# Key-value products of the next batch but one, moved from the first layer of the network to the second

## The chip, the cores and the metric

The kernel runs on one core of a Trainium2 chip. The metric is the device time of one execution, in microseconds. TensorE (PE) multiplies, VectorE (DVE) and ScalarE (ACT) work element by element, GpSimd (POOL) and SyncE (SP) here issue DMAs.

## The reference, cut to what matters

```python
def _attn_ref(q, k, v, g_norm):             # q, k, v: (8, 8, 576, 64)
    kv = np.einsum('bhsd,bhse->bhde', k, v)
    out = np.einsum('bhsd,bhde->bhse', q, kv)
    rms = np.sqrt(np.mean(out * out, axis=-1, keepdims=True) + 1e-06)
    return out / rms * g_norm

def _moe_ref(x, w_in, w_out):                # 4608 tokens, 512 -> 2048 -> 512
    h = x @ w_in
    g = h * (1.0 / (1.0 + np.exp(-1.702 * h)))
    return g @ w_out

# x = the attention's output of all batches, (batch, position) x (head, channel)
```

## The kernel before, in words

There are eight batches and nine tiles of 512 tokens. The loop at the end of the kernel runs over `t` from 0 to 8: pass `t` (called layer t here) puts tile `t` through both layers of the network, and beside it does the attention of batch `t + 1`. Tiles 0 to 7 hold the first 512 positions of a batch, tile 8 the last 64 positions of all of them. The weights stay in SBUF in f16.

**The network.** From layer 1 on both products are done as block products with seven multiplications instead of eight. The first half of a layer (`hid_seven`, `SevenIn`, L559) has 28 products of four 128x256 matmuls, in an order written out by hand: `SECOND` for layer 1, `LATER` for layers 2 to 6, `LAST_TWO` for 7 and 8. A step "21" is product 1 of group 2. The word "kv" in that list is the place of the key-value product. Product 1 of each group is followed by a copy of its bank to the bank on which product 2 accumulates (`snap`, L509, by ScalarE "A" or VectorE "D"). The gates, ScalarE's activations at L539, write `gT`; VectorE forms sums of operands (`xS` L491, `gS` L611). The second half (`Seven.run`, L681) has seven products of 16 matmuls in the order 1, 5, 6, 2, 7, 3, 4; a step of it is one matmul, so there are 112. Products 1, 6, 7 and 4 share one bank: after 1, 5 and 6 `keep` copies the state of a bank to `qf` (ScalarE, L648), and the next product goes on accumulating. `place` writes the output tile `osb` (VectorE L656; the last product's by ScalarE, L659).

**The attention.** For batches 2 to 7, `kv_all` makes k-transposed times v for four pairs of heads (40 matmuls, L238) into one bank and copies it to `kvd` in four copies of 64x256 (L509); before all are VectorE's. `kvd` has two buffers, by the parity of the batch. In the second half, behind step 15 in layers 2 to 6 (`'rows': (15, 15)`), `rows` makes two sets of 128 rows of q times kv with each call (L313, 16 matmuls a call), and ScalarE squares them. `add_up` sums the squares (VectorE, L329), `roots` takes roots (ScalarE, L338), `turn` scales and hands pairs of row sets to a DMA transpose into `xT`, the operand of the next layer. The last 64 positions go through `out`, `ss` and `apply`. The squares go through three buffers:

```python
sq = attn.tile([P, SM], F16, name="sq", tag="sq", bufs=3)
```

Each engine takes its instructions in the order in which the program was written; there is no scheduler. `at1(i, ...)` puts work behind step i of the first half, `at2(i, ...)` behind step i of the second; the late product "34" of `LATER`, with its gate, also stands behind step 15, ahead of the work put there. There is one buffer each for k and v (`kraw`, `vbuf`), so their next load, from GpSimd's queue, follows the product that reads them. q has two.

Of the kernel before, what the change touches and what calls it, by code (L numbers as in the profile page):

```python
# [7 lines left out]
F16 = mybir.dt.float16  # L8
# [4 lines left out]
P = 128  # L13
# [3 lines left out]
def kernel(  # L17
# [10 lines left out]
    nc = tc.nc  # L28

    B, H, S, D = q.shape  # L30
    DM = H * D
    DFF = moe_w_in.shape[1]
    NPAIR = H // 2
    FO = DFF // P
    KO = DM // P
    EPS = 1e-6
    SM = 512
    J = SM // P
# [10 lines left out]
    const = ctx.enter_context(tc.tile_pool(name="const", bufs=1))  # L49
    stage = ctx.enter_context(tc.tile_pool(name="stage", bufs=4))  # L50
    attn = ctx.enter_context(tc.tile_pool(name="attn", bufs=4))
# [18 lines left out]
    ident = const.tile([P, P], F16)  # L70
    ones2 = const.tile([P, P], F16)
    eps_t = const.tile([P, 1], F32)
    g_col = const.tile([P, 1], F32)
    w_in_sb = const.tile([P, KO, DFF], F16)
    w_out_sb = const.tile([P, FO, DM], F16)
# [32 lines left out]
    RW = J * D  # L108
    RS = H * RW

    def load_kv(b, h0=0, h1=H, rest=True):

        for n in "kv":
            nc.gpsimd.dma_start(  # L114
                out=kv_rows[n][:, h0 * RW : h1 * RW].rearrange("p (h x) -> p h x", x=RW),
                in_=srcs[n][b, h0:h1, 0:SM, :].rearrange("h (p j) d -> p h (j d)", j=J),
            )
        for n in "kv" if rest else "":
            nc.gpsimd.dma_start(
                out=kv_rows[n][0:R, RS : RS + H * D].rearrange("p (h d) -> p h d", d=D),  # L120
                in_=srcs[n][b, :, SM:S, :].rearrange("h p d -> p h d"),
            )

    def clear_rest():
        for n in "kv":
            nc.vector.memset(kv_rows[n][R:P, RS : RS + H * D], 0.0)
# [19 lines left out]
    for n in "kqv":  # L146
        if n != "q":
            rows = stage.tile([P, 6, 2 * P], F32, name="qf", tag="qf", bufs=2)
            rows = rows.rearrange("p h x -> p (h x)")[0:PE_]
# [8 lines left out]
        out=ident,  # L158
        in_=ident,
# [42 lines left out]
    xT = {}  # L202
# [8 lines left out]
    class Attention:  # L211
# [3 lines left out]
        def __init__(self, b):  # L215
            self.b, self.kb = b, kvb[b] if b < EARLY else kvd[b % 2]
            self.qT, self.o = {}, {}
            x = xpool.tile([P, KO * SM], F16, name="xT", tag="xT")
            if b < EARLY:
                self.x = xT[b] = x.rearrange("p (c n) -> p c n", c=KO)  # L220
            else:
                self.x = x.rearrange("p (m r) -> p m r", r=P)
                xT[b] = x.rearrange("p (j c r) -> p c j r", j=J, c=KO)
                self.x16 = attn.tile([P, J, DM], F16, name="x16", tag="x16", bufs=1)

        def kv(self, c):
            if c % self.KEEP == 0:
# [35 lines left out]
        def keep_kv(self, c0, c1):  # L263

            for half in range(2):
                to = slice(half * D, (half + 1) * D)
                for hl in range(2):
                    r = slice(hl * D, (hl + 1) * D)
                    copy(self.engine, self.kb[to, c0:c1, half, 1 - hl], self.kvp[r, c0:c1, :])

        def transpose_q(self):
            self.qTd = attn.tile([P, H * J // 2, P], F16, name="qTd", tag="qTd", bufs=1)
# [65 lines left out]
            nc.scalar.activation(s4, s4, AFT.Abs_reciprocal_sqrt, bias=eps_t, scale=1.0 / D)  # L338

        def turn(self, j):  # L340
            nc.vector.tensor_mul(
                self.x16[:, j, :].rearrange("p (h d) -> p h d", d=D),
                self.o[j][0].rearrange("p (h d) -> p h d", d=D),
                self.sum4[:, j, :].unsqueeze(2).to_broadcast([P, H, D]),
            )
            if j % 2:
                nc.sync.dma_start_transpose(
                    out=self.x[:, (j - 1) * KO : (j + 1) * KO, :],
                    in_=self.x16[:, j - 1 : j + 1, :].rearrange("p j n -> p (j n)"),
                )  # L350
# [157 lines left out]
    def copy(engine, to, src):  # L508
        (nc.vector.tensor_copy if engine == "D" else nc.scalar.copy)(to, src)  # L509
# [347 lines left out]
    for hl in range(2):  # L857
        r = slice(hl * D, (hl + 1) * D)
# [91 lines left out]
    def plan(t):  # L950
        return SECOND if t < EARLY else LATER if t < B - 1 else LAST_TWO
# [7 lines left out]
    for t in range(NT):  # L959
        b = t + 1  # L960
        u1, u2 = {}, {}

        def at1(i, f, *args):
            u1.setdefault(i, []).append(lambda: f(*args))

        def at2(i, f, *args):
            u2.setdefault(i, []).append(lambda: f(*args))  # L967

        def of(b, name, *args):
            return lambda: getattr(live[b], name)(*args)  # L970

        if t == 0:
            for l in range(2):
                at1(6, nc.vector.memset, kvd[l], 0.0)
            at1(7, of(0, "out", NPAIR))
            at1(7, scale_w_in, 0, 4)
            at1(7, w_in_sums, 0, 2)
            at1(8, start, 1)
            at1(12, scale_w_in, 4, 6)
            at1(12, w_in_sums, 2, 3)  # L980
            at1(13, load_q, 2)
            at2(4, setattr, a0, "ss_pool", Attention.ss_pool)
            at2(4, of(0, "ss", NPAIR, True))
            at2(4, of(0, "apply", NPAIR))
            at2(18, weight_sum, 0, 0, HF)
            at2(18, scale_w_in, 6, 8)
            at2(18, w_in_sums, 3, 4)
            for c in range(NPAIR):
                at1(12, of(1, "pack_q", c))
                at2(9 + 3 * c, of(1, "q", c))  # L990
                at2((36, 37, 49, 50)[c], of(1, "kv", c))
                at2((41, 43, 54, 55)[c], of(1, "out", c))
                at2((45, 50, 58, 60)[c], of(1, "ss", c))
                at2((48, 52, 58, 62)[c], of(1, "apply", c))
            for n in range(1, 4):
                at2(19, weight_sum, n, 0, 4)
                at2(38, weight_sum, n, 4, 6)
            at2(39, load_kv, 2, 0, H // 2, False)
            at2(51, clear_rest)
            at2(51, load_kv, 2, H // 2, H)  # L1000

            def first_sum():
                made[1] = Sums(1, xT[1])
                made[1].form(0)

            at2(55, first_sum)
        elif b < B:
            todo = plan(t)
            at1(todo.steps.index("kv"), of(b, "kv_all", todo.keep))
            if t == 1:  # L1010
                at1(5, start, b)
                at1(5, of(b, "transpose_q"))
                at1(4, nc.scalar.preload_act_table_set, "gelu_apprx_sigmoid_and_others")
                for n, i in ((1, 8), (2, 11), (3, 16)):
                    at1(i, weight_sum, n, 6, HF)
            if t + 2 < B:
                late = max(15, todo.steps.index("kv") + 1)
                at1(late, load_kv, t + 2)
                at1(late, load_q, t + 2)
                at2(100, start, t + 2)  # L1020
                at2(100, of(t + 2, "transpose_q"))
            at = todo.attn
            at2(at["table"], nc.scalar.preload_act_table_set, "abs_reciprocal_sqrt_and_small")
            for h in range(2):
                at2(at["roots"][h], of(b, "roots", h))
            for j in range(J):
                if j < J // 2:
                    at2(at["rows"][j], of(b, "rows", j))
                for name in ("add_up", "turn"):
                    at2(at[name][j], of(b, name, j))  # L1030
            at2(46, of(b, "out", NPAIR))
            at2(74, of(b, "ss", NPAIR))
            at2(80, of(b, "apply", NPAIR))
            at2(82, nc.scalar.preload_act_table_set, "gelu_apprx_sigmoid_and_others")
        elif t < B:
            for name in ("ss_pool", "rest_pool"):
                at2(16, setattr, live[1], name, (ps_a, "att"))
            at2(16, of(1, "out", NPAIR))
            at2(34, nc.scalar.preload_act_table_set, "abs_reciprocal_sqrt_and_small")
            at2(44, of(1, "ss", NPAIR))  # L1040
            at2(50, of(1, "apply", NPAIR))
            at2(52, nc.scalar.preload_act_table_set, "gelu_apprx_sigmoid_and_others")
        layers(t, u1, u2)
# [30 lines left out]
```

## Time and profile before

| | us |
|---|---|
| median of 3 runs | 260.13 (260.03 to 260.14) |
| profiled execution, its own time | 260.59 |
| its span, first to last instruction | 258.8 |
| TensorE busy | 251.4 (97%) |
| VectorE busy | 195.1 (75%) |
| ScalarE busy | 174.9 (68%) |
| GpSimd busy | 53.8 (21%) |

Busy times are shares of the span. A wait of one engine counts only if it lies on the chain that ended last. The chain here is 92% TensorE. Layer 2 lasts from 74.39 to 100.61 us, layer 3 to 126.82, and the layers up to 6 follow at the same distance; layers 7 and 8, without key-value products, are shorter up to the final store.

### The profile page before, as it was taken

What the parts mean: (1) busy time and instruction counts of PE and PEld (TensorE: products, weight loads), DVE (VectorE), ACT (ScalarE), POOL (GpSimd) and SP (SyncE); (2) the same over time, 40 slices, a digit from 0 to 9 for tenths busy, and PEclk for the clock granted to TensorE, in tenths of its full rate; (3) what the DMA queues carried; (4) which work ended last, traced back from release to release, by engine and by line L of the source; (5) the groups of instructions that cost most, each with busy time, mean ns of one, the idle gap of its engine ahead of it and who ended that gap; (6) DMA issues with size and microseconds to landing.
All of it is one profiled execution on the core that took longest, in us unless ns stands there. A gap on an engine that the chain in (4) does not pass through costs nothing.

```text
span 258.8 us, 6349 instructions
## 1 busy us (share of the span) xinstructions
PE 251.4 (97%) x2596; PEld 203.7 (79%) x2596; DVE 195.1 (75%) x351; ACT 174.9 (68%) x315; POOL 53.8 (21%) x81
## 2 busy tenths in 40 slices
PE   8889999999999999999999999999999999999993
PEld 2434454788888888888888888888888888888882
DVE  1565685899968896899689968996899687557842
ACT  3378734988749974997489748984798569737820
POOL 8773245107026001600170007000000000000001
PEclk9999999999999999999999999999999999999999
DMA  7999999999989957996799579947600610021005
GB/s 169 192 196 205 205 204 197 218 214 124 175 182 150 226 66 154 159 214 79 167 152 221 65 177 149 228 50 178 160 4 0 172 73 3 0 89 77 3 0 162
DMA packets 68559, 35.33 MB, mean 136 GB/s; under 512 B 37874, under 2 KB 65778, under 8 KB 68402
## 3 DMA queue, kind: packets, MB, share of 16 engines
q0 software_dynamic: 37520, 18.17, 54.4%
q1 hardware_dynamic: 30688, 16.36, 26.9%
q8 instruction: 20, 0.33, 0.5%
q10 hardware_dynamic: 322, 0.39, 0.4%
q14 instruction: 9, 0.07, 0.1%
HBM read 36.70 MB, written 9.44 MB: 178 GB/s over the span
## 4 chain that ended last, share of the span: by engine, by line
PE 92%; DMA 4%; DVE 1%; issue 0%; ACT 0%; POOL 0%
PE o L681 38%; PE h L559 38%; PE o L795 6%; PE hT L452 5%; DMA qraw<-in_q_dram 2%; DMA vbuf<-in_v_dram 2%; PE kvp L238 2%; PE outR L313 1%; PE ss L358 1%; PE kvp L250 0%; PE outT L283 0%; PE q L433 0%; DVE xT L368 0%; PE outT L287 0%; ACT rs L360 0%
## 5 line engine op out<-in xcount | busy, mean ns | idle before, releaser
L539 ACT ACTIVATE gT<-h 128x512 f16<-128x512 f32 x96 | 52.5, 602 | 5.4 <-PE h L559 5.4
L559 PEld LDWEIGHTS <-ws 128*128 128x128 f16 x512 | 50.1, 98 | 5.8
L681 PEld LDWEIGHTS <-gS 128*128 128x128 f16 x512 | 49.4, 98 | 6.2 <-DVE gS L611 0.3
L559 PE MATMUL h<-xS,ws 128*128 128x256 f16 x384 | 52.2, 273 | 0.0
L681 PE MATMUL o<-tw,gS 128*128 128x256 f16 x384 | 46.5, 273 | 0.0
L681 PEld LDWEIGHTS <-gT 128*128 128x128 f16 x384 | 37.6, 98 | 4.3
L559 PEld LDWEIGHTS <-w_in_sb 128*128 128x128 f16 x384 | 37.1, 98 | 4.7
L559 PE MATMUL h<-xT,w_in_sb 128*128 128x256 f16 x224 | 31.9, 273 | 0.0
L681 PE MATMUL o<-w_out_sb,gT 128*128 128x256 f16 x256 | 31.4, 273 | 0.0
L573 DVE TENSOR_TENSOR h<-h,s 128x512 f32<-128x512 f32 x32 | 22.2, 698 | 6.8 <-PE h L559 5.5
L575 DVE TENSOR_TENSOR s<-h,s 128x512 f32<-128x512 f32 x32 | 22.1, 692 | 4.1 <-PE h L559 3.3
L656 DVE TENSOR_TENSOR osb<-o,qf 128x512 f32<-128x512 f32 (+1 forms) x25 | 16.7, 668 | 11.2 <-PE o L681 8.3
L114 POOL DMA_DIRECT2D kraw<-in_k_dram x7 | 6.0, 853 | 90.6 <-PE kvp L238 86.4
L611 DVE TENSOR_TENSOR gS<-gT 128x512 f16<-128x512 f16 (+2 forms) x32 | 21.3, 686 | 0.6 <-ACT gT L539 0.6
L539 ACT ACTIVATE gT<-s 128x512 f16<-128x512 f32 x32 | 19.8, 628 | 2.6 <-DVE s L575 2.6
L714 POOL DMA_DIRECT2D out_dram<-osb x2 | 1.1, 562 | 92.0 <-DVE osb L656 92.0
L559 PE MATMUL h<-xS,w_in_sb 128*128 128x256 f16 x128 | 18.9, 273 | 0.0
L360 ACT ACTIVATE rs<-ss,eps_t 128x512 f32<-128x512 f32 (+1 forms) x16 | 9.2, 581 | 13.8 <-PE ss L358 13.7
L967 ACT ACT_TABLE_LOAD x14 | 18.0, 1283 | 0.2
L648 ACT COPY qf<-o 128x512 f32<-128x512 f32 (+1 forms) x26 | 14.2, 547 | 4.5 <-PE o L681 4.3
L329 DVE TENSOR_REDUCE sum<-sq 128x8 f32<-128x512 f16 x24 | 15.3, 678 | 2.5 <-ACT sq L323 2.5
L509 ACT COPY h<-h 128x512 f32<-128x512 f32 x27 | 15.7, 586 | 2.1 <-PE h L559 2.0
(100 smaller groups left out, 362.9 us busy)
## 6 DMA issues: line engine op xcount, KB each, us to landing
out_dram<-osb SPq DMA_DIRECT2D x10, 512.0 KB, 3.6
kraw<-in_k_dram POOLq DMA_DIRECT2D x5, 512.0 KB, 9.2
vbuf<-in_v_dram POOLq DMA_DIRECT2D x5, 512.0 KB, 12.1
qraw<-in_q_dram POOLq DMA_DIRECT2D x3, 512.0 KB, 13.2
qbuf<-in_q_dram POOLq DMA_DIRECT2D x3, 512.0 KB, 13.4
out_dram<-osb SPq DMA_DIRECT2D x6, 192.0 KB, 6.2
w_in_sb<-in_moe_w_in_dram POOLq DMA_DIRECT2D x2, 512.0 KB, 10.7
w_out_sb<-in_moe_w_out_dram POOLq DMA_DIRECT2D x2, 512.0 KB, 15.3
```

The costliest lines, as they stand in the source:

```text
L329: nc.vector.tensor_reduce(out=self.sum4[:, j, :], in_=self.o[j][1].rearrange("p (x d) -> p x d", d=D), op=ALU.add, axis=mybir.AxisListType.X,)
L509: (nc.vector.tensor_copy if engine == "D" else nc.scalar.copy)(to, src)
L539: nc.scalar.activation(self.gT[:, to, n * TH : (n + 1) * TH], src, AFT.Gelu_apprx_sigmoid)
L559: nc.tensor.matmul(bank[name][:, a], w, x, start=(p in (1, 5) and a == 0 and k == 0), stop=(k == KH - 1), skip_group_check=True,)
L573: nc.vector.tensor_add(bank["z"], bank["x"], self.s5)
L575: nc.vector.tensor_add(self.s5, bank["x"], self.s5)
L611: op(s[:, n, lo], a, b)
L648: nc.scalar.copy(self.kept[as_][:, m], ps)
L656: nc.vector.tensor_add(o, ps, self.kept[with_][:, m])
L681: nc.tensor.matmul(o, a, w, start=(p in (1, 2, 5) and i == 0 and (mo == 0 or split)), stop=(i == HF - 1), skip_group_check=True,)
L795: nc.tensor.matmul(os[mo], gT[:, fo, mo * P : (mo + 1) * P], w_out_sb[:, fo, :], start=(fo == 0), stop=(fo == FO - 1),)
L967: u2.setdefault(i, []).append(lambda: f(*args))
```

## The change

The key-value product of batch 2 stays in the first half of layer 1. That of batch 3 moves to step 95 of the second half of layer 1; those of batches 4 to 7 move to step 15 of the second half of layers 2 to 5, ahead of the rows of batches 3 to 6. In the first halves of layers 2 to 6 nothing stands at "kv" any more. The four copies take letters of their own, "DDDD", "DADA" and "ADDD", instead of one letter for all. k of the next batch is loaded right behind the product; v, the rests and q wait on GpSimd behind `after_turn`, a copy of one element of the transposed rows. The squares' sum of the last positions, its application and the table load move from steps 74, 80 and 82 to 82, 88 and 90. The buffer `x16` is taken in the first `turn` instead of with the batch's object.

```diff
-    def load_kv(b, h0=0, h1=H, rest=True):
+    def load_kv(b, h0=0, h1=H, rest=True, main="kv"):
-        for n in "kv":
+        for n in main:
             nc.gpsimd.dma_start(
...
+    def after_turn(b):
+        nc.gpsimd.tensor_copy(out=mark, in_=xT[b].rearrange("p c j r -> p j c r")[0:1, J - 1, KO - 1, 0:1])
...
-                    copy(self.engine, self.kb[to, c0:c1, half, 1 - hl], self.kvp[r, c0:c1, :])
+                    copy(
+                        self.engine[2 * half + hl],
+                        self.kb[to, c0:c1, half, 1 - hl],
+                        self.kvp[r, c0:c1, :],
+                    )
...
-            at1(todo.steps.index("kv"), of(b, "kv_all", todo.keep))
+            at = todo.attn
             if t == 1:
+                at1(todo.steps.index("kv"), of(b, "kv_all", "DDDD"))
...
+                at1(22, load_kv, 3)
+                at1(22, load_q, 3)
+                at2(95, start, 3)
+                at2(95, of(3, "kv_all", "DADA"))
+                at2(96, load_kv, 4)
+                at2(96, load_q, 4)
+            elif t + 2 < B:
+                at2(at["rows"][0], start, t + 2)
+                at2(at["rows"][0], of(t + 2, "kv_all", "ADDD"))
+                if t + 3 < B:
+                    at2(at["rows"][0], load_kv, t + 3, 0, H, False, "k")
+                    at2(101, after_turn, b)
+                    at2(101, load_kv, t + 3, 0, H, True, "v")
+                    at2(101, load_q, t + 3)
             if t + 2 < B:
-                late = max(15, todo.steps.index("kv") + 1)
-                at1(late, load_kv, t + 2)
-                at1(late, load_q, t + 2)
-                at2(100, start, t + 2)
                 at2(100, of(t + 2, "transpose_q"))
...
-            at2(74, of(b, "ss", NPAIR))
-            at2(80, of(b, "apply", NPAIR))
-            at2(82, nc.scalar.preload_act_table_set, "gelu_apprx_sigmoid_and_others")
+            at2(82, of(b, "ss", NPAIR))
+            at2(88, of(b, "apply", NPAIR))
+            at2(90, nc.scalar.preload_act_table_set, "gelu_apprx_sigmoid_and_others")
```

More of the change, by code (lines that the diff above doesn't have):

```diff
@@ L72 @@
     eps_t = const.tile([P, 1], F32)
+    mark = const.tile([1, 1], F16)
     g_col = const.tile([P, 1], F32)
@@ L223, in __init__ @@
                 xT[b] = x.rearrange("p (j c r) -> p c j r", j=J, c=KO)
-                self.x16 = attn.tile([P, J, DM], F16, name="x16", tag="x16", bufs=1)
         def kv(self, c):
@@ L340, in turn @@
         def turn(self, j):
+            if j == 0:
+                self.x16 = attn.tile([P, J, DM], F16, name="x16", tag="x16", bufs=1)
             nc.vector.tensor_mul(
@@ L1015 @@
                     at1(i, weight_sum, n, 6, HF)
+                at1(22, load_kv, 3)
[12 more added lines that the diff above has]
+                    at2(101, load_q, t + 3)
             if t + 2 < B:
-                late = max(15, todo.steps.index("kv") + 1)
-                at1(late, load_kv, t + 2)
-                at1(late, load_q, t + 2)
-                at2(100, start, t + 2)
                 at2(100, of(t + 2, "transpose_q"))
-            at = todo.attn
             at2(at["table"], nc.scalar.preload_act_table_set, "abs_reciprocal_sqrt_and_small")
```

## The prediction

> **What bounds the kernel now.** I read the page first, then the stretches of one layer each, then who made TensorE wait.
>
> ```profile
> span 258.8 us, 6349 instructions
> PE 251.4 (97%) x2596; PEld 203.7 (79%) x2596; DVE 195.1 (75%) x351; ACT 174.9 (68%) x315; POOL 53.8 (21%) x81
> PEclk9999999999999999999999999999999999999999
> 100.61:126.82 26.21, 26.21 (x303) 23.18 (x302) 22.01 (x38) 19.41 (x36) 5.27 (x7) 1.00 1.04 153
> 126.82:153.04 26.22, 26.22 (x304) 23.20 (x302) 22.02 (x38) 19.41 (x36) 5.27 (x7) 1.00 0.99 151
> ...
> PE kv L250 <- DMA vbuf<-in_v_dram: 0.9, 2, 0.7
> PE hT L452 <- DVE xT L368: 0.3, 1, 0.3
> ```
>
> A middle layer lasts 26.2 us, and TensorE is busy in all of it (the first number after the stretch is its length, the second TensorE's busy time). The waits for TensorE name only lines of the start (L250, L452). So a layer is a queue of matmuls with no hole. The change adds and drops no matmul: six key-value products are made before and after. The time can only fall by cheaper neighbours in that queue, and it rises by every hole that opens. The question is therefore which matmul now comes before its operands are ready.
>
> The stretches that matter, from the timeline of one layer (start, length, engine, line; a matmul's length holds its drain, so starts are what to read):
>
> ```profile
> 100.44 1.04 PE L559 MATMUL h<-xT,w_in_sb 128*128 128x256 f16 x8
> 101.41 0.82 PE L238 MATMUL kvp<-vbuf,kraw 128*64 128x64 f16 x40
> 102.17 0.61 PE L559 MATMUL h<-xT,w_in_sb 128*128 128x256 f16 x4
> ...
> 114.84 0.60 PE L559 MATMUL h<-xS,w_in_sb 128*128 128x256 f16 x4
> 115.37 0.64 PE L313 MATMUL outR<-kvd,qTd 64*128 64x64 f16 x32
> 115.94 3.56 PE L681 MATMUL o<-tw,gS 128*128 128x256 f16 x31
> ...
> 121.31 1.36 PE L681 MATMUL o<-tw,gS 128*128 128x256 f16 x11
> 102.23 11.02 PE h L559 x100
> ```
>
> The last row, from the chain, gives 0.11 us for one 128x256 matmul.
>
> **Part 1: the key-value product leaves the first half of layers 2 to 6.** It stood behind the first two products of the plan, "21 01 kv 22". It filled 0.76 us (102.17 - 101.41) and some 0.10 us of entry: eight matmuls from 100.44 last 0.87, and the product began at 101.41 instead of 101.31. Product 22 accumulates onto a bank that ScalarE first fills with a copy of product 21 (the plan's snap for group 2 is "A"). ScalarE's rows at that place:
>
> ```profile
> 100.64 0.58 ACT L659 COPY osb<-o 128x512 f32<-128x512 f32 x1 [2.27 <-PE o L681]
> 101.13 0.59 ACT L509 COPY h<-h 128x512 f32<-128x512 f32 x1
> ```
>
> The copy that 22 needs (L509) stands behind the copy of the old layer's last output (L659), which itself waits for that layer's last matmul. It ends at 101.13 + 0.59 = 101.72. Before, 22 came at 102.17 and the key-value product hid this. Now 22 follows directly at 101.31, while the copy still ends at 101.72; with 0.04 us for the handover (the rows show 0.02 to 0.04 from one engine's end to another's start) TensorE stands until 101.76, a hole of 0.45 us. It occurs in layers 2 to 6: 5 x 0.45 = 2.25 us. What else is late there? VectorE loses its four casts (1.7 us), so its sums come no later.
>
> **Part 2: the product stands ahead of the rows in layers 2 to 5.** The rows began at 115.37 and took 0.57 us. In their place come 40 small matmuls. What stays is the body, and the step from one small kind to the other replaces the step back to a large matmul and the entry to the rows. No row shows that step. It lies between nothing (the spacing inside either group) and a full entry of 0.10 more than usual; the exit from the key-value product is 0.76 less 20 pairs of about 0.03, some 0.13. I take 0.11 us saved a layer, nearer to the entry seen at 101.41; the ends are 0 and 0.2. The Trainium skill, "TensorE: Matmul & The Clock Gate", section "Part 3: Packing small matmuls — row/col tiling", says that a weight load overlaps running matmuls only where the row groups differ; the product uses all 128 rows, so by it nothing would be saved and the sum would be 0.44 us higher. The rows inside the product speak for more overlap than that: 40 weight loads and 40 matmuls, all on the same 128 rows, start within 0.63 us.
>
> What follows on the other engines is the larger matter. The rows of before:
>
> ```profile
> 115.52 0.60 ACT L539 ACTIVATE gT<-h 128x512 f16<-128x512 f32 x1
> 116.01 2.08 ACT L323 ACTIVATE sq<-outR 128x512 f16<-128x512 f32 x4
> 118.10 1.28 ACT L967 ACT_TABLE_LOAD   x1
> 119.40 0.31 ACT L338 ACTIVATE sum<-sum,eps_t 128x16 f32<-128x16 f32 x1
> 119.61 0.57 ACT L648 COPY qf<-o 128x512 f32<-128x512 f32 x1
> 120.08 0.31 ACT L338 ACTIVATE sum<-sum,eps_t 128x16 f32<-128x16 f32 x1
> 120.28 0.37 ACT L301 ACTIVATE sq<-outT 128x256 f16<-128x256 f32 x1
> 120.55 0.58 ACT L648 COPY qf<-o 128x512 f32<-128x512 f32 x1
> ...
> 115.48 0.69 DVE L611 TENSOR_TENSOR gS<-gS,gT 128x1024 f16<-128x1024 f16 x1
> 116.65 1.28 DVE L329 TENSOR_REDUCE sum<-sq 128x8 f32<-128x512 f16 x2 [0.47 <-ACT sq L323]
> 117.84 0.68 DVE L611 TENSOR_TENSOR gS<-gT,gS 128x1024 f16<-128x1024 f16 x1
> 102.46 1.72 DVE L509 CAST kvd<-kvp 64x256 f16<-64x256 f32 x4
> L648 ACT COPY qf<-o 128x256 f32<-128x256 f32 x4 | 1.5, 371 | 0.8 <-PE o L681 0.8
> L238 PE MATMUL kvp<-vbuf,kraw 128*64 128x64 f16 x240 | 4.9, 197 | 0.0
> ```
>
> ScalarE is full from 115.52 to 121.13, the end of the last copy to qf. TensorE needs that copy: the product that begins at 121.31 goes on accumulating in the bank which it reads. So before there are 0.18 us to spare. Now, with the layer's clock up to 115.37 as before:
>
> 1. The product's last matmul starts at 115.37 + 0.63 and ends 0.20 later, 116.20.
> 2. The four copies out of its bank carry the letters "ADDD". In the order of the changed program ScalarE's copy is first, and VectorE's first one waits for it. ScalarE on this shape is not in the trace; its nearest row, 256 columns, is 0.37 us, its 512-column copy 0.58. With 0.37: 116.23 to 116.60.
> 3. VectorE's three: 3 x 0.43 (1.72 / 4) from 116.63, so it is free at 117.92. Queued behind them are a sum for the second half (L611, 0.60 to its successor) and the first reduction of squares, which so begins at 118.52 and ends at 119.20. It was at 116.65.
> 4. Only three buffers hold squares ("bufs=3"). ScalarE's fourth square must wait for that reduction: 119.25 instead of 117.45 (116.01 + 3 x 0.48).
> 5. Behind this on ScalarE stand the table load, both roots and both copies to qf, the rest as full as before: 121.13 - 117.45 = 3.68 us, so the last copy ends at 122.93, and TensorE may go on at 122.97.
> 6. TensorE itself would be there at 121.31 + 0.75 = 122.06. Hole: 0.91 us, in four layers 3.64 us.
>
> The turned rows are late by the same 1.8 us, but the layer's end moves by 0.75 + 0.91, so the transposes keep their distance to the next layer within 0.2 us. With ScalarE at 0.58 in step 2 a layer costs 0.2 more.
>
> **Part 3: batch 3's product near the end of layer 1, and the loads.** Layer 1 gains 0.86 us, which layer 2's first half loses: nothing in sum. Its copies alternate VectorE and ScalarE, each behind the other, some 1.8 us beside 17 matmuls (1.9 us); cover that just suffices. The squares' sum, its application and the table load move eight steps back, into ScalarE's idle end of the layer; nothing.
>
> ```profile
> 103.39 0.90 POOL L114 DMA_DIRECT2D vbuf<-in_v_dram  x1
> 121.05 2.62 SPq L347 DMA_TRANSPOSE xT<-x  x2
> vbuf<-in_v_dram POOLq DMA_DIRECT2D x5, 512.0 KB, 12.1
> xT<-x SPq DMA_TRANSPOSE x12, 3.2
> ```
>
> The next k is asked for behind the product (116.2), and v, both rests and q wait on GpSimd behind a one-element copy that waits for the last transpose: second issue about 122.4 + 1.8, landing 3.2 later, 127.4. Nothing else is queued on GpSimd but these loads. v lands 12.1 later at about 139.6, the rests within 1 us. The product wants them one layer on, at 115.37 + 26.2 + 1.3 = 142.9. Some 2 us to spare; nothing. Batch 4's, asked for at the end of layer 1, have 16 us.
>
> **Sum:** 2.25 + 3.64 - 0.44 = +5.45 us. Against the profiled execution's 260.59 us (span 258.8 and 1.8 around it) that is 266.0; that execution is 0.46 above the median of the runs, so 265.6 by the median.
>
> **The rivals.** One of them needs two groups of matmuls of the same shape, from the start and from the first layer (count, busy time, mean ns):
>
> ```profile
> L843 PE MATMUL idle<-kvb 128*128 128x512 f16 x16 | 6.5, 570 | 1.3 <-DVE one_t L192 1.3
> L795 PE MATMUL o<-w_out_sb,gT 128*128 128x512 f16 x64 | 16.6, 380 | 0.0
> ```
>
> - *Only part 1 opens a hole* (13%): ScalarE keeps up because a step of the chain in part 2 is shorter than its row. For it: 0.91 us is the end of six steps. Against: the 0.18 us of slack is small beside the 1.1 us that the reduction falls behind the rows. 2.25 - 0.44 = +1.8: 261.9.
> - *Faster* (5%): no hole at all, only cheaper neighbours. It decides where the copy of product 21 ends by 101.31 instead of 101.72, and the fourth square does not wait. -0.44: 259.7. Against: the copy cannot start before the old layer's last output, whose place is unchanged.
> - *Loads late* (8%): v shares the DMA engines with the transposes of q from its start. If landing takes 4 us more than 12.1, the product stands 2 us in three layers: +6 more, 271. For it: 2 us is not much; against: in before the same transposes already ran beside k and v.
> - *The clock falls* (2%): the first matmuls took 570 ns, the same shape later 380, half as long again. If that came back for a product of 16 matmuls after each of the nine holes, each 0.05 us longer, it is 9 x 16 x 0.05 = +7 beside the holes themselves, 273. Against: PEclk stayed at 9 through the early waits for v. The Trainium skill, "TensorE: Matmul & The Clock Gate", section "A second HAM failure mode: psum-queue depth-cycling", tells of short idles between groups that made the clock fall and rise; this trace shows none.
> - *No effect* (2%): gains and holes cancel, 260.1.
>
> **How the numbers follow.** The forecast has 70%. Its own ends: part 2 at 0.75 to 1.2 a layer (handovers of 0.02 or 0.10, ScalarE's copy 0.37 or 0.58), savings 0.8 or 0, part 1 at 0.42 to 0.46: +4.3 to +7.2, 264.4 to 267.4. The range takes in the first rival and leaves out the others: 261.8 to 267.6. About 0.2%, 0.5 us, is what a measurement of this kernel can tell from none: faster 0.05, same 0.03, slower 0.92.
>
> **What would show it.** Right: TensorE waits for ScalarE's L519 copy at the second product of layers 2 to 6 (about 0.45 us each) and for the copy to qf in layers 2 to 5 (about 0.9), the fourth square starts when the first reduction ends, and layers 2 to 5 last about 27.5 us. Wrong: layers of 26.2 us or less, a busy TensorE at both places, or waits of the product for its loads.

## The result, and the profile after

| | before | after |
|---|---|---|
| median, us | 260.13 (260.03 to 260.69, 4 runs) | 266.27 (265.81 to 266.49, 4 runs) |
| profiled execution, its own time | 260.59 | 265.81 |
| its span | 258.8 | 264.0 |

The ratio is 1.0227 with a 95% interval of 1.0202 to 1.0251: the changed kernel is slower by 5.3 to 6.5 us. The forecast was 265.6, in a range of 261.8 to 267.6.

Line numbers grow by up to ten in the changed kernel: L559 is now L569, L681 L691, L509 L519, L313 L321, L329 L337, L611 L621, L648 L658, L238 L242. The page of after:

```profile
span 264.0 us, 6352 instructions
PE 251.2 (95%) x2596; PEld 203.3 (77%) x2596; DVE 193.0 (73%) x345; ACT 177.8 (67%) x321; POOL 54.4 (21%) x84
PEclk9999999999999999999999999999999999999999
```

The stretches of layers 2, 3 and 6 (length first, then TensorE's busy time):

```profile
74.48:102.05 27.57, 26.46 (x303) 23.18 (x301) 21.67 (x38) 19.98 (x38) 5.60 (x9) 1.00 0.98 149
102.05:129.62 27.57, 26.46 (x303) 23.18 (x301) 21.16 (x36) 19.94 (x37) 4.59 (x7) 1.00 1.16 145
184.75:210.56 25.81, 25.52 (x263) 22.56 (x261) 20.83 (x36) 19.41 (x36) 0.00 (x0) 1.00 0.36 85
```

Who made TensorE wait (us in total, times, longest), middle layers:

```profile
PE o L691 <- ACT qf L658: 3.3, 4, 0.8
PE h L569 <- ACT h L519: 1.4, 5, 0.3
```

TensorE's work is the same 251 us. It now waits nine times in the middle layers, four times for the copy to qf and five times for ScalarE's copy of product 21, and never for a load there. (A wait in this list is shorter than the hole it stands for, because a matmul's drain counts as busy: eight matmuls whose spacings add up to 0.87 us have a row of 1.04, so about 0.17 us.) On the chain that ended last TensorE's share falls from 92% to 80%; ScalarE now has 8% of it and VectorE 4%. Layers 2 to 5 grew from 26.22 to 27.57 us; layer 6, which lost its product and makes no new one, shrank to 25.81. (In the views of before the first matmul of layer 3 starts at 100.44 us, while its stretch is cut at 100.61; the lengths of the layers are the same either way.)

The first hole, at the start of layer 3, in the timeline of TensorE:

```profile
102.05 1.04 PE L569 MATMUL h<-xT,w_in_sb 128*128 128x256 f16 x8
103.38 0.60 PE L569 MATMUL h<-xT,w_in_sb 128*128 128x256 f16 x4 [0.29 <-ACT h L519]
```

And of ScalarE:

```profile
102.25 0.58 ACT L669 COPY osb<-o 128x512 f32<-128x512 f32 x1 [1.39 <-PE o L691]
102.73 0.59 ACT L519 COPY h<-h 128x512 f32<-128x512 f32 x1
```

Product 22 could have come at 102.05 + 0.87 = 102.92 and came at 103.38, 0.06 after the end of the copy (102.73 + 0.59): a hole of 0.46 us.

The second hole, in the second half of the same layer, on TensorE:

```profile
116.57 0.82 PE L242 MATMUL kvp<-vbuf,kraw 128*64 128x64 f16 x40
117.32 0.64 PE L321 MATMUL outR<-kvd,qTd 64*128 64x64 f16 x32
117.89 3.56 PE L691 MATMUL o<-tw,gS 128*128 128x256 f16 x31
...
121.52 1.91 PE L691 MATMUL o<-w_out_sb,gT 128*128 128x256 f16 x16
124.25 1.91 PE L691 MATMUL o<-tw,gS 128*128 128x256 f16 x16 [0.82 <-ACT qf L658]
```

On VectorE:

```profile
117.84 1.30 DVE L519 CAST kvd<-kvp 64x256 f16<-64x256 f32 x3 [1.19 <-ACT kvd L519]
119.17 0.69 DVE L621 TENSOR_TENSOR gS<-gS,gT 128x1024 f16<-128x1024 f16 x1
119.78 1.27 DVE L337 TENSOR_REDUCE sum<-sq 128x8 f32<-128x512 f16 x2
```

On ScalarE:

```profile
117.44 0.36 ACT L519 CAST kvd<-kvp 64x256 f16<-64x256 f32 x1
117.76 1.57 ACT L331 ACTIVATE sq<-outR 128x512 f16<-128x512 f32 x3
120.55 0.60 ACT L331 ACTIVATE sq<-outR 128x512 f16<-128x512 f32 x1 [1.21 <-DVE sum L337]
121.17 1.28 ACT L977 ACT_TABLE_LOAD   x1
122.46 0.31 ACT L346 ACTIVATE sum<-sum,eps_t 128x16 f32<-128x16 f32 x1
122.67 0.57 ACT L658 COPY qf<-o 128x512 f32<-128x512 f32 x1
123.14 0.31 ACT L346 ACTIVATE sum<-sum,eps_t 128x16 f32<-128x16 f32 x1
123.35 0.37 ACT L309 ACTIVATE sq<-outT 128x256 f16<-128x256 f32 x1
123.61 0.58 ACT L658 COPY qf<-o 128x512 f32<-128x512 f32 x1
```

VectorE stands still for 1.19 us until ScalarE's cast of the product is done, casts until 119.14, sums, and ends the first reduction only at about 120.5. ScalarE's fourth square waits 1.21 us for it, and the copy to qf behind it ends at 124.19. TensorE could have gone on at 121.52 + 16 x 0.109 = 123.27 and goes on at 124.25: 0.98 us. (0.109 us is the spacing of 128x256 matmuls: 0.87 for eight.)

The layers add up. 4 x (27.57 - 26.22) = 5.40, layer 6 gives back 0.41, and layer 1 gains 0.86 (the product at its end); together 5.85 us. From the holes it is the same: 5 x 0.46 + 4 x 0.98, less some 0.09 saved in each of four layers. In these two profiled executions layer 1 began 0.6 us earlier in after, which is why their spans differ by 5.2 only.

### The profile page after: what moved, and what is told of

It is laid out like the page before. It is cut to its first block, busy times and chain, and to the rows that moved or that the text cites. A ratio compares the mean times of both kernels' runs of the same rounds, so it can differ in the third digit from the quotient of the medians.

```text
span 264.0 us, 6352 instructions
## 1 busy us (share of the span) xinstructions
PE 251.2 (95%) x2596; PEld 203.3 (77%) x2596; DVE 193.0 (73%) x345; ACT 177.8 (67%) x321; POOL 54.4 (21%) x84
## 4 chain that ended last, share of the span: by engine, by line
PE 80%; ACT 8%; DVE 4%; DMA 4%; issue 1%; POOL 0%; ACTq 0%
PE h L569 36%; PE o L691 30%; PE o L805 5%; PE hT L462 5%; DMA vbuf<-in_v_dram 2%; DMA qraw<-in_q_dram 2%; ACT L977 2%; DVE kvd L519 2%; PE kvp L242 2%; ACT osb L669 1%; DVE gS L621 1%; ACT h L519 1%; PE ss L368 1%; ACT sum L346 1%; ACT qf L658 1%
## 5 line engine op out<-in xcount | busy, mean ns | idle before, releaser
L691 PEld LDWEIGHTS <-gS 128*128 128x128 f16 x512 | 49.0, 98 | 10.6 <-issue 4.0
L569 PEld LDWEIGHTS <-ws 128*128 128x128 f16 x512 | 50.1, 98 | 5.8
L569 PE MATMUL h<-xS,ws 128*128 128x256 f16 x384 | 52.2, 273 | 0.0
L691 PE MATMUL o<-tw,gS 128*128 128x256 f16 x384 | 45.8, 273 | 3.3 <-ACT qf L658 3.3
L569 PEld LDWEIGHTS <-w_in_sb 128*128 128x128 f16 x384 | 37.4, 98 | 6.9 <-issue 2.3
L691 PEld LDWEIGHTS <-gT 128*128 128x128 f16 x384 | 37.5, 98 | 4.3
L569 PE MATMUL h<-xT,w_in_sb 128*128 128x256 f16 x224 | 31.8, 273 | 1.4 <-ACT h L519 1.4
L583 DVE TENSOR_TENSOR h<-h,s 128x512 f32<-128x512 f32 x32 | 22.2, 697 | 13.5 <-PE h L569 12.4
L691 PE MATMUL o<-w_out_sb,gT 128*128 128x256 f16 x256 | 31.4, 273 | 0.0
L621 DVE TENSOR_TENSOR gS<-gT 128x512 f16<-128x512 f16 (+2 forms) x32 | 21.2, 684 | 0.6 <-ACT gT L549 0.6
L569 PE MATMUL h<-xS,w_in_sb 128*128 128x256 f16 x128 | 18.9, 273 | 0.0
L658 ACT COPY qf<-o 128x512 f32<-128x512 f32 (+1 forms) x26 | 14.2, 546 | 4.5 <-PE o L691 4.4
L519 ACT COPY h<-h 128x512 f32<-128x512 f32 x27 | 15.7, 586 | 2.1 <-PE h L569 2.0
L569 PE MATMUL h<-xT,ws 128*128 128x256 f16 x112 | 16.8, 273 | 0.0
```

What stands on the lines that cost most here:

```text
L569: nc.tensor.matmul(bank[name][:, a], w, x, start=(p in (1, 5) and a == 0 and k == 0), stop=(k == KH - 1), skip_group_check=True,)
L583: nc.vector.tensor_add(bank["z"], bank["x"], self.s5)
L621: op(s[:, n, lo], a, b)
L658: nc.scalar.copy(self.kept[as_][:, m], ps)
L691: nc.tensor.matmul(o, a, w, start=(p in (1, 2, 5) and i == 0 and (mo == 0 or split)), stop=(i == HF - 1), skip_group_check=True,)
```

## The experiments

Each run is set against runs of the kernel before on the same chip; that kernel's median is 260.16 us for the three runs with the exchange of products 05 and 22, and 260.06 to 260.08 for the other eight.

**The first hole alone, in the kernel before.**

```diff
-        "21 01 kv 22 05 25 06 11 02 15 26 03 16 12"
+        "21 01 22 kv 05 25 06 11 02 15 26 03 16 12"
```

> The kernel before with two neighbours swapped in the plan of layers 2 to 6: "21 01 22 kv" instead of "21 01 kv 22"; nothing else. Theory of two holes: only the first hole opens, 5 x 0.45 = +2.2 us, 262.4. Rival, that the hole needs the rest of the change (GpSimd's marker, later transposes): no change, 260.1.

Measured: 262.52 us, ratio 1.009 (1.007 to 1.011). TensorE at the start of layer 3:

```profile
100.49 1.04 PE L559 MATMUL h<-xT,w_in_sb 128*128 128x256 f16 x8
101.82 0.60 PE L559 MATMUL h<-xT,w_in_sb 128*128 128x256 f16 x4 [0.29 <-ACT h L509]
```

ScalarE:

```profile
101.17 0.59 ACT L509 COPY h<-h 128x512 f32<-128x512 f32 x1
```

The stretch of layer 3:

```profile
100.49:127.16 26.67, 26.38 (x304) 23.19 (x301) 22.11 (x38) 19.60 (x36) 5.27 (x7) 1.00 0.98 150
```

One exchange of neighbours, with nothing else of the change, makes the same hole (101.82 against 101.36) and a layer 0.45 us longer. The key-value product had been the filler there.

**The second hole alone taken away.** The changed kernel, with the products at step 95:

```diff
-                at2(at["rows"][0], start, t + 2)
-                at2(at["rows"][0], of(t + 2, "kv_all", "ADDD"))
+                at2(95, start, t + 2)
+                at2(95, of(t + 2, "kv_all", "DADA"))
                 if t + 3 < B:
-                    at2(at["rows"][0], load_kv, t + 3, 0, H, False, "k")
+                    at2(96, load_kv, t + 3, 0, H, False, "k")
```

> The changed kernel with the key-value products of batches 4 to 7 at step 95 of the second half (copies "DADA", k loaded at step 96), as batch 3's stands already. Theory of two holes: the hole at the copy to qf (0.98 us in four layers) shuts, the 0.11 us of cheaper neighbours go too: 266.3 - 3.9 + 0.4 = 262.8. Rival, that the longer layers come from the loads split around the transposes or from contention: they are still split, so the time stays near 266.

Measured: 262.59 us, ratio 1.0093 (1.0072 to 1.0114). The wait for the copy to qf is gone from the list, the one for ScalarE's L519 copy is still there five times, and layers 2 to 5 last 26.66 us: before's 26.22 and the first hole.

**Shutting the first hole, first try.** A product put between 01 and 22:

```diff
-        "21 01 kv 22 05 25 06 11 02 15 26 03 16 12"
+        "21 01 11 kv 22 05 25 06 02 15 26 03 16 12"
```

> The changed kernel with one more product between the first two and product 22 in layers 2 to 6 ("21 01 11 kv 22" instead of "21 01 kv 22 05 25 06 11"). Theory of two holes: ScalarE's copy of product 21 is now done when 22 comes, so the first hole (0.46 us in five layers) shuts and the time falls by 2.0 to 2.3 us to about 264.0; the hole at the copy to qf stays at 0.98. Rival, that TensorE pays for something else at the layer's start (late transposes of the rows, changed clock): the time stays at 266.3 and the same idle time shows one product later.

Measured: 270.35 us, ratio 1.0395 (1.0376 to 1.0414). Neither came: product 22 no longer waits (the first row of the layer holds 21, 01, 11 and 22 without a gap), but product 25, two places behind it, does, for longer. TensorE from the start of layer 3:

```profile
102.81 1.92 PE L569 MATMUL h<-xT,w_in_sb 128*128 128x256 f16 x16
104.57 0.60 PE L569 MATMUL h<-xS,ws 128*128 128x256 f16 x4
106.34 1.03 PE L569 MATMUL h<-xS,ws 128*128 128x256 f16 x8 [1.17 <-ACT gT L549]
```

ScalarE:

```profile
105.21 0.58 ACT L519 COPY s<-h 128x512 f32<-128x512 f32 x1 [0.26 <-PE h L569]
105.69 0.60 ACT L549 ACTIVATE gT<-h 128x512 f16<-128x512 f32 x1
```

Product 11 opens two banks, one of them for the copy of its own state, and now does so before product 25 instead of behind it. In the kernel's text that one, those of products 21 and 01 for the same purpose, and the bank of product 25 come from one pool of three (`ps_h`). So all three are taken when 25 wants one, and 25 waits for the gate (to 106.29) that frees the oldest. A hole of 1.33 us (106.34 against 104.57 + 0.44) replaced one of 0.46. The expectation had looked at the copy alone and not at the banks.

**The same with the products at step 95.**

> Both edits: the extra product ahead of 22 and the product at step 95. Theory of two holes: both shut, the time is that of the kernel before within 0.5 us (260.1 to 260.6). If something else in the change costs (loads, GpSimd's wait, moved sums), what stays above 260.1 is its price.

Measured: 267.17 us, ratio 1.0268 (1.0252 to 1.0283), with the wait for the gate five times and no other in these layers. The expectation failed for the same reason; the run says nothing of a rest.

**Shutting the first hole, second try.** Product 05, whose bank is in another pool, exchanged with 22:

```diff
-        "21 01 kv 22 05 25 06 11 02 15 26 03 16 12"
+        "21 01 kv 05 22 25 06 11 02 15 26 03 16 12"
```

> The changed kernel with products 05 and 22 exchanged in layers 2 to 6 ("21 01 kv 05 22 25"). Product 05 opens a bank of another pool than the one that stood in the way in the run with product 11, and its operand, the first sum of the rows, ends at 130.43 where 05 would start at 130.49 (profile of after). Theory of two holes: the first hole shuts and no other opens, 5 x 0.46 = -2.3 us, 264.0. Rival, that whatever comes third waits: no gain, 266.3.

Measured: 264.54 us (263.75 to 266.41), ratio 1.0179 (1.0149 to 1.0210). The wait for the L519 copy is gone, that for the copy to qf stays four times, and layer 3 lasts 27.14 us, 0.43 less than in after. The profiled execution is the slowest of the four: it began layer 1 only at 49.88 us, with a granted clock of 0.93 up to there, where after's began it at 47.15 with 1.00. Its layers 1 to 6 are 2.2 us shorter than after's in sum, near the 2.3 expected. The median is only 1.7 us lower; what the other three executions spent ahead of layer 1 is not on record.

**Both holes shut.** This exchange and step 95:

> The exchange of 05 and 22, and the key-value products at step 95. Theory of two holes: both shut, and what is left of the change (split loads, GpSimd's marker, moved sums, batch 3's place) costs nothing: 260.1, within 0.5 us of the kernel before. A rest above 260.6 would be a third cost.

Measured: 260.36 us (12 runs), ratio 1.0008 (0.9998 to 1.0018). TensorE at the start of layer 3:

```profile
100.47 1.04 PE L569 MATMUL h<-xT,w_in_sb 128*128 128x256 f16 x8
101.34 0.60 PE L569 MATMUL h<-xS,ws 128*128 128x256 f16 x4
101.79 0.60 PE L569 MATMUL h<-xT,w_in_sb 128*128 128x256 f16 x4
```

ScalarE:

```profile
101.15 0.59 ACT L519 COPY h<-h 128x512 f32<-128x512 f32 x1
```

The stretches of layers 3 and 6:

```profile
100.47:126.70 26.23, 26.23 (x304) 23.21 (x302) 21.25 (x37) 20.34 (x39) 5.43 (x9) 1.00 1.10 154
179.16:204.53 25.37, 25.37 (x263) 22.57 (x261) 20.92 (x37) 19.63 (x37) 0.00 (x0) 1.00 0.36 75
```

The copy ends at 101.74 and product 22 begins at 101.79: the filler is just long enough. The layers are as full as before, layer 6 loses what layer 1 gains, and the interval leaves at most 0.5 us. So the split loads, GpSimd's marker, the moved sums and batch 3's place cost nothing that shows.

**One part alone.** The kernel before with the last positions' sum, its application and the table load eight steps later.

> The kernel before with one part of the change alone: the squares' sum of the last positions, its application and the table load eight steps later. Theory of two holes: this part lies in ScalarE's idle time, 260.1 within 0.3 us. Rival: it delays ScalarE at the layer's end and with it the copy that product 22 needs, +0.5 us or more.

Measured: 260.06 us (10 runs), ratio 1.000 (0.999 to 1.001). This part is free.

**What the second hole is made of.** Three edits of the changed kernel: four buffers for squares (`bufs=4`), the copies "DDDD", the copies "AAAA".

> The changed kernel with four buffers for the squares instead of three. Theory, that the three buffers make the hole: the fourth square no longer waits for VectorE's first reduction, the copy to qf is 1.2 us earlier and the hole at it shuts, -3.9 us, 262.4. Rival, that VectorE's backlog itself makes it: the second root, which stands ahead of that copy on ScalarE, still waits for the fourth reduction (end at 122.84 in the profile of after), so the copy ends only about 0.25 us earlier and the hole shrinks from 0.98 to about 0.7, -1 us, 265.2.

> The changed kernel with all four copies of a key-value product on VectorE ("DDDD") in layers 2 to 5. Theory, that VectorE's backlog sets the hole: VectorE starts at the product's end and not after ScalarE's copy, needs 4 x 0.43 = 1.72 instead of 0.40 + 3 x 0.43 = 1.69, so the hole stays at 0.98, no change (266.2 to 266.5). Rival, that ScalarE's own copy makes ScalarE late: its 0.36 us go, and the hole shrinks by 0.3 us in four layers, 265.0.

> The changed kernel with all four copies on ScalarE ("AAAA") in layers 2 to 5. Theory, that VectorE's backlog sets the hole: VectorE is free, ScalarE takes 4 x 0.32 = 1.3 us ahead of the squares, the fourth square starts some 0.2 to 0.3 us earlier than in after, the hole falls from 0.98 to about 0.65, -1.3 us, 265.0. Rival, that ScalarE's added work sets it: three more copies on ScalarE make the hole 0.9 us longer, +3.6 us, 270.

Measured: 266.01 (ratio 1.0227, 1.0212 to 1.0242), 266.20 (1.0236, 1.0220 to 1.0251) and 265.73 us (1.0218, 1.0202 to 1.0233). With four buffers the fourth square waits no more, but the second root does, and then TensorE waits a second time. The run with four buffers, ScalarE:

```profile
118.03 2.06 ACT L331 ACTIVATE sq<-outR 128x512 f16<-128x512 f32 x4
...
123.14 0.31 ACT L346 ACTIVATE sum<-sum,eps_t 128x16 f32<-128x16 f32 x1 [0.95 <-DVE sum L337]
```

VectorE:

```profile
125.54 0.68 DVE L621 TENSOR_TENSOR gS<-gT,gS 128x1024 f16<-128x1024 f16 x1
```

TensorE:

```profile
121.78 1.91 PE L691 MATMUL o<-w_out_sb,gT 128*128 128x256 f16 x16
124.24 1.91 PE L691 MATMUL o<-tw,gS 128*128 128x256 f16 x16 [0.55 <-ACT qf L658]
126.27 0.50 PE L691 MATMUL o<-w_out_sb,gS 128*128 128x256 f16 x3
```

The hole at the copy to qf is 0.71 us instead of 0.98 (124.24 against 123.53), as the rival said, and 0.28 us opens ahead of 126.27, where the next product wants VectorE's last sum (125.54 + 0.68 = 126.22). Layer 3 is as long as in after, 27.57. So the three buffers only carried the delay; behind them stands VectorE, late by its casts. "DDDD" changes nothing that can be measured (layers of 27.60): VectorE starts earlier but has one cast more. "AAAA" makes layers 2 to 5 0.14 us shorter (27.43), less than the 0.3 expected. ScalarE in that run:

```profile
117.29 1.50 ACT L519 CAST kvd<-kvp 64x256 f16<-64x256 f32 x4
118.81 2.06 ACT L331 ACTIVATE sq<-outR 128x512 f16<-128x512 f32 x4
```

Its casts follow each other at 0.38 us, four in 1.50, not at 0.32. The squares no longer wait for VectorE, but now begin behind all four casts. Whichever engine casts, some 1.5 us of casts stand between the rows and the copy.

**Beside the rows, with the other work moved away.** Besides the exchange of 05 and 22 and four buffers for squares:

```diff
-        {0: ((0, 8, 2),), 16: ((4, 8, 1),), 22: ((4, 8, 3),), 58: ((0, 4, 3),)},
+        {0: ((0, 8, 2),), 16: ((4, 8, 1),), 22: ((4, 8, 3),), 32: ((0, 4, 3),)},
-        {'rows': (15, 15), 'add_up': (17, 20, 24, 28), 'table': 24, 'roots': (28, 39), 'turn': (35, 38, 46, 48)},
+        {'rows': (15, 15), 'add_up': (17, 20, 24, 28), 'table': 24, 'roots': (28, 47), 'turn': (35, 38, 47, 48)},
-            at2(82, of(b, "ss", NPAIR))
-            at2(88, of(b, "apply", NPAIR))
-            at2(90, nc.scalar.preload_act_table_set, "gelu_apprx_sigmoid_and_others")
+            at2(92, of(b, "ss", NPAIR))
+            at2(98, of(b, "apply", NPAIR))
+            at2(100, nc.scalar.preload_act_table_set, "gelu_apprx_sigmoid_and_others")
```

> The changed kernel with the product still beside the rows, 05 and 22 exchanged, four buffers for squares, the second pair of roots behind the copy to qf (step 47), the last sum for the second half ahead of the turned rows (step 32) and the squares' sum of the last positions at steps 92 to 100. Theory, that the second hole is VectorE's and ScalarE's work between the rows and the copies: the copy to qf no longer waits for it and that hole shuts; VectorE stays late by 1.3 us of copies, so a smaller wait for its output copy comes near the layer's end, 0.2 to 0.3 us in four layers: 261 to 262. Rival, that the product beside the rows costs TensorE itself (switching between matmul kinds): the time stays at 264 or above.

Measured: 263.41 us (262.20 to 264.53), ratio 1.0140 (1.0116 to 1.0164); above the expected 261 to 262, though the hole at the copy to qf is gone as the theory said. Layer 3:

```profile
101.97:128.44 26.47, 26.30 (x303) 23.18 (x301) 21.41 (x37) 20.15 (x37) 5.44 (x8) 1.00 1.01 152
```

The waits of TensorE in the middle layers:

```profile
PE h L569 <- ACT h L519: 1.0, 1, 1.0
PE o L691 <- DVE osb L666: 0.7, 4, 0.2
```

What the expectation missed is one wait of 1.0 us at the start of layer 2: the table load, moved to step 100, now stands in layer 1 behind the casts of batch 3 and ahead of the copy that product 22 needs. ScalarE there:

```profile
74.42 1.28 ACT L977 ACT_TABLE_LOAD   x1
75.72 0.59 ACT L669 COPY osb<-o 128x512 f32<-128x512 f32 x1
76.20 0.59 ACT L519 COPY h<-h 128x512 f32<-128x512 f32 x1
```

The layers 1 to 6 of this execution are together 2.4 us longer than before's, which gives about 262.5. The rival's price, a cost of the product on TensorE itself, does not appear: layers 3 to 5 are only 0.25 to 0.37 us longer than in before, and one wait each for the output copy (0.2 us, and the drain) stands for most of that. The profiled execution is the fastest of the four, and the 0.9 us more of the median, like the spread among the four, was not explained. No version beats the kernel before; the one with both holes shut equals it.

## Why the prediction was right

- *TensorE is full, so every hole counts.* Right: its busy time is 251.2 us against 251.4, and the layers' growth equals the holes.
- *Part 1, 0.45 us in five layers.* Measured 0.46 in after, and made by itself in the kernel before, 0.45 a layer. The handover was 0.06 us, not 0.04.
- *Part 2, 0.91 us in four layers.* Measured 0.98. Each of the six steps is in the rows: ScalarE's cast, 0.36 for the assumed 0.37; VectorE's three casts at 0.43; the sum; the reduction; the fourth square behind it; the copy to qf, which waits on. The difference of 0.07 lies in handovers over several engines.
- *0.11 us saved where the two small kinds meet.* The rows began 0.75 us after the product (117.32 - 116.57), where in before the way back to a large matmul took 0.76 and the rows' entry 0.09 more. By these steps 0.10 is saved, by the layers' growth 0.09 (0.46 + 0.98 - 1.35). The Trainium skill's rule on weight loads and row groups ("TensorE: Matmul & The Clock Gate", "Part 3: Packing small matmuls — row/col tiling"), taken alone, would have saved nothing; this trace does not agree with it at that place. The same section also says that a load to the background weight buffer is pulled ahead of running matmuls, which the prediction did not weigh.
- *Part 3, nothing.* Right for the moved sums (run by themselves) and for all the rest together. The loads were closer than worked out. v landed 9.3 us after its issue in the median, sooner than the 12.1 taken; but its issue came 12.4 to 13.9 us after the start of the product and not 12.0, and the rests landed up to about 3.7 us after v and not within 1. In layer 4 the last rest landed at 142.66, 1.5 us ahead of the product at 144.14.
- *The sum*, 5.45, against 6.14 between the medians (5.3 to 6.5) and 5.85 by the layers. Part 2 was too small by 0.28 in all and part 1 by 0.05, and the saving was too large by 0.08. Together these are the 0.4 us between sum and layers. The 0.3 us between layers and medians lies within the interval and is not located. The upper end of the forecast's own ends adds to 7.1 us, not 7.2; the measured time lies below either.
- *Rivals.* Part 1 alone would have given 261.9 with the saving beside the rows. The run at step 95 keeps only that hole and has no such saving, so its figure is 260.1 + 2.3 = 262.4; it measured 262.59. Late loads and a lower clock did not come: PEclk stays at 9 through the holes, which at most last 1 us, and the granted clock of layers 2 to 6 is 1.00.

## What to carry to other kernels

A short piece of work between two steps that depend on each other through a slower engine is also a filler; before moving it, look for what must be done within its time (here a 0.59 us copy queued behind another). Work put where two helper engines are full and wait for each other is paid by the engine that waits for them: here some 1.5 us of casts cost TensorE 0.98 us. A new filler has to be checked for the banks it opens as well as for its operands.

## What the runs showed of the hardware

k's load of 512 KB lands 5.9 us after its issue when it runs alone behind the product beside the rows. In before it took 9.2, with v's load issued right behind it and the transposes of q running; which of the two made the difference was not separated. The rests of k and v, 64 KB each, issued right behind v beside those transposes, land up to 2.3 us after the load ahead of them. ScalarE's cast of 64x256 from a bank took 0.37 us, VectorE's 0.42, and back to back 0.38 and 0.43: ScalarE needs about an eighth less for this shape.
